# Attention and two expert layers on one core: the second half of a weight product moved behind the first layer and made from float32r parts

## The chip, the cores and the metric

The kernel runs on one core of a Trainium2 chip. The metric is the device time of one execution in microseconds (us). The kernel before was run three times: 860.75, 860.82 and 862.73 us, median 860.82 us.

A core has a matrix engine (TensorE, PE in the profile; its weight loads are PEld), VectorE (DVE), ScalarE (ACT), GpSimd (POOL) and SyncE (SP), which here issues all the transfers. Each engine takes its instructions in the order in which they were written and waits on semaphores for the others.

## The reference

```python
def _attn_ref(q, k, v):                      # 4 batches, 8 heads, 576 positions, 64 wide
    scores = np.matmul(q, k.transpose(0, 1, 3, 2)) / np.sqrt(D)
    # causal mask: 32 wide for heads 0..3, 128 wide with a step of 4 for heads 4..7
    scores = np.where(masks[None], scores, -1000000000.0)
    attn = np.exp(scores - np.max(scores, axis=-1, keepdims=True))
    attn = attn / (np.sum(attn, axis=-1, keepdims=True) + 1e-09)
    return np.matmul(attn, v)

def _moe_ref(x, w1, w2, w3, w_out):          # x 2304x512; w1, w2 512x1024; w3 1024x1024; w_out 1024x512
    a = x @ w1
    b = x @ w2
    h = a * b @ w3
    return h @ w_out

def _moe2_ref(x, w_in, w_out, a, b):         # w_in 512x2048, w_out 2048x512
    h = x @ w_in
    P = a[0] + a[1] * h + a[2] * h * h + a[3] * h * h * h
    Q = 1.0 + np.abs(b[0]) * np.abs(h) + np.abs(b[1]) * h * h
    return (P / (Q + 1e-06)) @ w_out
```

The three are chained: attention gives x, the first expert layer gives a new x, the second the output. The weights arrive as 64-bit words, two int32 each, which are put together on the chip.

## The kernel before

The 2304 tokens go through phase 1 (attention and the first expert layer) in eight blocks of 288 (k = 0..7) and through phase 2 (the second expert layer) in five blocks of up to 512.

Most products run on float32r parts: a number x is cut into a high part (a ScalarE cast) and a low part (VectorE, x minus high), and three products (high by high, high by low, low by high) are summed in PSUM. A plain float32 product needs no parts; it shows in the trace as two matmul records for each instruction.

Phase 1 does not keep w3 and w_out apart. It first forms W3o = w3 w_out (1024 by 512) in two halves of 512 rows, each four PSUM banks, summed over eight slabs j. For each j there are two steps (`w3_mm`, e = 0, 1) of two plain float32 matmuls of 128x512. Each finished bank is then cut into parts (`w3_high`, `w3_low`). The rest is:

- **Slabs.** A weight slab (128x512 words, 512 KB) is loaded, scaled by ScalarE (`scale`, L215), then shifted, signed and completed by VectorE (L219, L223, L234). The eight slabs of w_out and the sixteen of w3 stay whole; the sixteen of w1 and w2 are also cut into parts (`high`, `low`, L241 and L245).
- **Attention.** 32 groups, eight for each pair of blocks. A group is a score product (L316), six masks (L332), six exponentials (L340), sums and a reciprocal (L345, L347), a division on POOL (L352), transposes (L359), a product with v (L374), and its cut into parts (L393, L397).
- **First layer** (`l1`, L426): for each m of 8 and both of w1 and w2, twelve matmuls of 128x288 into the two banks `ab`; then a copy and a product (`l1_copy`, `l1_mul`). The slabs m of w1 and w2 serve blocks 0 and 1 one after the other, so that each slab is used as it comes.
- **Second layer** (`l2`, L472): the product by W3o, for each n of 4 a bank `acc` of 24 matmuls. Block 0's products stay in SBUF as parts (`l1_high`, and `l1_low` on POOL); block 1's go to DRAM (`p_store`), come back (`p_load`) and are cut then (`p_high`, `p_low`).
- **Weights of phase 2.** 32 slabs are put together beside phase 1 and stored in DRAM.

The order of phase 1 is made by a planner (`Plan.order`): every step has an engine, a duration, predecessors, buffers and a due time, and each engine takes the ready step that is due first. The due times come from `main_jobs`, the order of TensorE's products. There it says: first half of W3o, four slabs of the second half, then m by m the first layer of blocks 0 and 1 with one further slab of the second half after each of the first four m, then `l2(0)`, `l2(1)`, then blocks 2 to 7. A first-layer product of block 0 waits for the eight groups of attention of its two blocks and for its slab.

Phase 2 is written out: `step(i)` issues a product with w_in, its rational function, and the product with w_out of four steps earlier. Block 7's second layer is done there (`tail`), after step 0.

Of the kernel before, what the change touches and what calls it, by code (L numbers as in the profile page):

```python
# [18 lines left out]
P = 128  # L19
# [26 lines left out]
W12SLOT = ("p0", "p1", "p2", "p3", "w34", "w35", "w30", "w31",  # L46
           "wo0", "wo1", "wo2", "wo3", "wo4", "wo5", "wo6", "wo7")
# [3 lines left out]
W3BANKS = (("acc", "acc", "ab", "ab"), ("acc", "acc", "sc", "sc"))  # L51
# [4 lines left out]
W3_AT = 4  # L56
PACE = 1.12
B_FROM = 120.0

# [118 lines left out]
class Kern:  # L178
# [28 lines left out]
    def part(self, pool, tag):  # L207
        return pool.tile([P, 2, DM], F32R, tag=tag, bufs=1, name="w")
# [30 lines left out]
    def high(self, s):  # L239
        s["w"] = self.part(s["pool"], s["tag"])  # L240
        self.nc.scalar.copy(s["w"][:, 0], s["x"])  # L241
# [158 lines left out]

    def w3_mm(self, half, j, e):
        if j == 0 and e == 0:
            self.wo[half] = [self.bank(t) for t in W3BANKS[half]]
        w3, wout = self.w3T[half, j]["x"], self.wout[j]["x"]
        for i in (2 * e, 2 * e + 1):
            self.nc.tensor.matmul(self.wo[half][i], w3[:, i * P:(i + 1) * P], wout, start=j == 0,  # L406
                                  stop=j == M1 - 1)
# [42 lines left out]
    def p_store(self, m):  # L450
        self.nc.sync.dma_start(out=self.pd[m // 2, :, m % 2], in_=self.pp[1, m])

    def p_load(self, i):
        w = self.p2[1, i] = self.gp.tile([P, 2, 2, TA], F32R, tag="g", bufs=5, name="pp")
        self.nc.sync.dma_start(out=w[:, 1].bitcast(F32), in_=self.pd[i])

    def p_high(self, i):
        w = self.p2[1, i]
        self.nc.scalar.copy(w[:, 0], w[:, 1].bitcast(F32))

    def p_low(self, i):
        w = self.p2[1, i]
        self.nc.vector.tensor_tensor(out=w[:, 1], in0=w[:, 1].bitcast(F32), in1=w[:, 0].bitcast(F32),
                                     op=ALU.subtract)

    def l2(self, k, n, e):
        if e == 0:
            self.l2_acc[k, n] = self.bank("acc")
        acc = self.l2_acc[k, n]
        for m in range(4 * e, 4 * e + 4):  # L470
            for a, c in ((0, 0), (1, 0), (0, 1)):
                self.nc.tensor.matmul(acc[:, 0:TA], self.W3o[m][0][:, a, n * P:(n + 1) * P],  # L472
                                      self.p2[k, m // 2][:, c, m % 2],
# [30 lines left out]
    def phase1(self):  # L504
        io, Q, Pp = self.io, self.Q, self.Pp
        for n in ("qT", "kT", "vb", "sc", "pr", "sm", "pt", "pT", "xt", "xs", "ab", "a_sb", "pp", "p2",
                  "w3T", "wout", "wo", "w12", "l2_acc", "x2", "bs", "braw", "win", "wo2"):
# [13 lines left out]
        for job in self.main_jobs():  # L521
            T[job] = t
            t += 1.72 if job[0] == "w3" else 1.57 * PACE
# [4 lines left out]
        for G in range(2 * B * HP):  # L528
            u, half = divmod(G, 2)
            b, hp = divmod(u, HP)  # L530
            if half == 0:
                lb = [buf(x) for x in ("qT", "kT", "vb")]
                lq = add("SP", 0.9, self.att_load_q, u, new=lb[0:1])
                lk = add("SP", 0.95, self.att_load_k, u, new=lb[1:2])
                lv = add("SP", 1.2, self.att_load_v, u, new=lb[2:3])
# [5 lines left out]
            due = T["l1", 2 * b, 0, 0] - 1 - (2 * HP - 1 - G % (2 * HP)) * (GAP if b else GAP0)  # L541
# [23 lines left out]
        def words(src, pool, tag, raw=True):  # L565
# [3 lines left out]
            ld = add("SP", 1.6, self.load, s, new=[wb])  # L569
# [13 lines left out]
        keys = [x for j in range(M1) for x in (("o", j), (0, j))] + [(1, j) for j in range(M1)]  # L583
        homes, prev = {}, {}
        for g, j in keys:
            tag = f"wo{j // 2}" if g == "o" else f"wo{4 + j // 2}"
# [4 lines left out]
            s, a = unsplit(src, n, homes[hk], xbs[hk], Q, tag, prev[hk])  # L591
# [7 lines left out]
        w3o, last = [], []  # L599
        for g in range(2):  # L600
            wb = [buf(x) for x in W3BANKS[g]]
            for j in range(M1):
                for e in range(2):
                    f = j == 0 and e == 0
                    a = add("PE", 1.72, self.w3_mm, g, j, e, after=[ready["o", j], ready[g, j]] + last[-1:],
                            new=wb if f else [], use=([] if f else wb) + [xbs["o", j // 2], xbs[g, j // 2]],
                            due=T["w3", g, j, e])
                    last = [a]
            for i in range(4):
                hi = add("ACT", 0.6, self.w3_high, g, i, after=last + w3o[-1:], new=[buf(f"p{4 + 4 * g + i}")],  # L610
                         use=[wb[i]], due=T["w3", g, M1 - 1, 1] + 2 + 0.6 * i)
                w3o.append(hi)
                last.append(add("DVE", 0.66, self.w3_low, g, i, after=[hi], use=[wb[i]],
                                due=T["w3", g, M1 - 1, 1] + 3 + 0.6 * i))
            lows = last[1:] if g == 0 else lows + last[1:]
            last = last[:1]
# [17 lines left out]
        def l1_jobs(k, m):  # L634
# [13 lines left out]
            if k == 1:  # L648
                kept[m] = add("SP", 0.45, self.p_store, m, after=[mu], use=tb[1:], due=d + 4)
# [8 lines left out]
        def back_jobs():  # L658
            pl, gbs = parts.setdefault(1, ([], []))
            for i in range(M1 // 2):  # L660
                gb = buf("g")
                d = T["l2", 1, 0, 0] - 12 + 1.5 * i
                a = add("SP", 0.95, self.p_load, i, new=[gb], due=d,
                        after=[kept[2 * i], kept[2 * i + 1]] + parts[0][0][-1:])
                a = add("ACT", 0.67, self.p_high, i, after=[a], use=[gb])
# [355 lines left out]
```

## Time and profile before

| | |
|---|---|
| median of 3 runs | 860.82 us |
| the profiled execution, time | 860.87 us |
| its span, first to last instruction | 859.1 us |
| TensorE busy | 838.7 us (98%) |
| VectorE busy | 578.5 us (67%) |
| ScalarE busy | 533.7 us (62%) |
| mean granted TensorE clock | 0.998 |

The profiled execution is one run of the program; 1.8 us of its time lie outside its span. Busy time is the time in which an engine executes; a line such as L426 is the line of the source from which the instruction was issued. A tile is named without its number, and its four uses as PSUM bank are `ab`, `acc`, `sc` and `px`, two banks each.

### The profile page before, as it was taken

How to read it: one execution, taken by the hardware profiler on the slowest of the kernel's cores; microseconds unless marked ns; L12 is line 12 of the kernel's file. 1: busy time of each engine (PE TensorE's matmuls, PEld its weight loads, DVE VectorE, ACT ScalarE, POOL GpSimd, SP SyncE). 2: the span in 40 equal slices, each digit the busy share in tenths (PEclk: the TensorE clock that was granted, in tenths of full speed). 3: DMA queues.
4: the chain of work that ended last, by engine and by line, in shares of the span. 5: the costliest groups of instructions: out<-in, count | busy, mean ns of one | idle time of the engine just before them, and what ended most of it. 6: DMA issues, size and time to landing. Idle time of an engine off the chain costs nothing.

```text
span 859.1 us, 14509 instructions
## 1 busy us (share of the span) xinstructions
PE 838.7 (98%) x5216; PEld 718.1 (84%) x5216; DVE 578.5 (67%) x1264; ACT 533.7 (62%) x1202; POOL 328.1 (38%) x305
## 2 busy tenths in 40 slices
PE   5989999999999999999999999999999999999998
PEld 2546799889999999999998778888888888888886
DVE  6889997776775223321225887788777877787775
ACT  3785557663566334632235877777777777787773
POOL 1240023132143213312123655565556655564443
PEclk9999999999999999999999999999999999999999
DMA  9787346876775112042334000010000100001112
GB/s 357 257 334 238 114 135 220 291 251 221 256 256 166 54 56 77 19 150 104 105 107 145 25 14 24 12 38 14 26 13 24 37 13 13 13 25 42 43 45 93
DMA packets 43464, 95.06 MB, mean 111 GB/s; under 512 B 4736, under 2 KB 13952, under 8 KB 43392
## 3 DMA queue, kind: packets, MB, share of 16 engines
q1 hardware_dynamic: 43392, 94.13, 32.5%
q8 instruction: 41, 0.67, 0.3%
q14 instruction: 31, 0.25, 0.1%
HBM read 71.57 MB, written 22.54 MB: 110 GB/s over the span
## 4 chain that ended last, share of the span: by engine, by line
PE 89%; ACT 5%; DVE 4%; DMA 1%; issue 1%; POOL 0%; SPq 0%; ACTq 0%; POOLq 0%; DVEq 0%
PE ab L426 24%; PE acc L851 11%; PE sc L851 11%; PE ab L801 11%; PE px L801 10%; PE acc L472 10%; PE acc L406 3%; PE sc L316 2%; PE px L374 2%; PE sc L406 2%; PE px L359 2%; PE ab L406 1%; DMA words<-moe_w_in 1%; ACT pr L340 1%; DVE v L829 1%
## 5 line engine op out<-in xcount | busy, mean ns | idle before, releaser
L426 PE MATMUL ab<-xs,w 128*128 128x288 f32 x1536 | 215.9, 298 | 0.2 <-ACT xs L393 0.2
L426 PEld LDWEIGHTS ab<-xs,w 128*128 128x128 f32 x1536 | 205.8, 188 | 5.4 <-issue 1.7
L812 POOL TENSOR_TENSOR y<-y,v 128x512 f32<-128x512 f32 x72 | 95.8, 1331 | 143.1 <-ACT y L811 142.8
L352 POOL TENSOR_TENSOR pr<-pr,sm 96x384 f32<-96x384 f32 x64 | 56.3, 898 | 175.0 <-DVE sm L347 124.3
L851 PE MATMUL acc<-w,gg 128*128 128x512 f32 x432 | 109.7, 391 | 1.4 <-ACT r L822 1.4
L472 PE MATMUL acc<-pp,w 128*128 128x288 f32 x768 | 109.2, 298 | 1.2 <-DVE XS L909 1.0
L447 POOL TENSOR_TENSOR pp<-p,pp 128x288 fp32r<-128x288 f32 x56 | 48.1, 860 | 162.7 <-ACT pp L443 156.1
L851 PE MATMUL sc<-w,gg 128*128 128x512 f32 x432 | 109.4, 390 | 0.0
L472 PEld LDWEIGHTS acc<-pp,w 128*128 128x128 f32 x768 | 103.3, 188 | 2.9 <-PE acc L472 1.2
L801 PE MATMUL ab<-XS,w 128*128 128x512 f32 (+1 forms) x480 | 105.4, 370 | 0.0
L801 PE MATMUL px<-XS,w 128*128 128x512 f32 (+1 forms) x480 | 105.3, 370 | 0.0
L838 POOL TENSOR_TENSOR gg<-t,gg 128x512 fp32r<-128x512 f32 x72 | 93.7, 1302 | 10.7 <-ACT gg L837 10.1
L801 PEld LDWEIGHTS px<-XS,w 128*128 128x128 f32 x480 | 83.8, 188 | 16.4
L801 PEld LDWEIGHTS ab<-XS,w 128*128 128x128 f32 x480 | 83.7, 188 | 16.2
L851 PEld LDWEIGHTS acc<-w,gg 128*128 128x128 f32 x432 | 80.7, 188 | 19.2 <-ACT r L822 1.8
L851 PEld LDWEIGHTS sc<-w,gg 128*128 128x128 f32 x432 | 80.8, 188 | 17.3
L436 DVE TENSOR_TENSOR p<-a_sb,ab 128x288 f32<-128x288 f32 x64 | 28.9, 452 | 81.2 <-PE ab L426 68.4
L340 ACT ACTIVATE pr<-pr,sm 96x128 f32<-96x128 f32 x192 | 74.8, 395 | 9.0 <-DVE sm L332 9.0
L215 ACT ACTIVATE dec<-words 128x512 f32<-128x512 f32 x72 | 47.9, 676 | 37.9 <-DMA words<-moe_w_out 11.8
L829 DVE SCALAR_TENSOR_TENSOR v<-y,cs,r 128x512 f32<-128x512 f32 x72 | 71.2, 989 | 0.0
L821 ACT ACTIVATE r<-y,cs 128x512 f32<-128x512 f32 x72 | 52.2, 726 | 14.5 <-POOL y L812 14.3
L811 ACT ACTIVATE y<-v,cs 128x512 f32<-128x512 f32 x72 | 58.8, 817 | 2.4
(76 smaller groups left out, 1152.9 us busy)
## 6 DMA issues: line engine op xcount, KB each, us to landing
words<-moe_w SPq DMA_DIRECT2D x32, 512.0 KB, 5.3
words<-moe_w_out SPq DMA_DIRECT2D x24, 512.0 KB, 4.5
words<-moe_w_in SPq DMA_DIRECT2D x16, 512.0 KB, 4.1
wd<-dec SPq DMA_DIRECT2D x32, 256.0 KB, 2.3
c<-wd SPq DMA_DIRECT2D x32, 256.0 KB, 2.6
vb<-v SPq DMA_DIRECT2D x16, 384.0 KB, 3.7
XS<-x2d SPq DMA_DIRECT2D x6, 1024.0 KB, 7.6
kT<-k SPq DMA_DIRECT2D x16, 304.0 KB, 4.2
```

Of the source, the lines that this page charges most:

```text
L340: self.nc.scalar.activation(out=pr[:, i], in_=pr[:, i], func=AF.Exp, scale=-1.0, bias=sm[:, 0, i:i + 1], accum_out=sm[:, 1, i:i + 1])
L352: self.nc.gpsimd.tensor_tensor(out=pr[:, i], in0=pr[:, i], op=ALU.mult, in1=sm[:, 2, i].unsqueeze(2).to_broadcast([QT, 3, P]))
L406: self.nc.tensor.matmul(self.wo[half][i], w3[:, i * P:(i + 1) * P], wout, start=j == 0, stop=j == M1 - 1)
L426: self.nc.tensor.matmul(t[:, 0:TA], w[:, s[0], c * P:(c + 1) * P], xs[:, s[1], c, tok], start=n == 0, stop=n == 11)
L472: self.nc.tensor.matmul(acc[:, 0:TA], self.W3o[m][0][:, a, n * P:(n + 1) * P], self.p2[k, m // 2][:, c, m % 2], start=m == 0 and (a, c) == ...
L801: nc.tensor.matmul(t[:, e * nt:(e + 1) * nt], w[:, s[0], c * P:(c + 1) * P], XS[blk][:, s[1], c], start=n == 0, stop=n == 11)
L811: nc.scalar.activation(out=w, in_=v, func=AF.Identity, scale=self.b1, bias=self.b0)
L812: nc.gpsimd.tensor_tensor(out=w, in0=w, in1=v, op=ALU.mult)
L821: nc.scalar.activation(out=r, in_=yy[i][1], func=AF.Ln, bias=self.c1)
L829: nc.vector.scalar_tensor_tensor(out=v, in0=w, scalar=self.c1, in1=r, op0=ALU.add, op1=ALU.mult)
L838: nc.gpsimd.tensor_tensor(out=t[:, 1], in0=u, in1=t[:, 0].bitcast(F32), op=ALU.subtract)
L851: nc.tensor.matmul(acc[g, blk][tk], t[:, s[0], j:j + P], w[:, s[1]], start=f + e == 0 and s == (0, 0), stop=f + e == FG - 1 and s == (1, 0))
```

## The change

The second half of W3o is no longer computed in plain float32 before and between the first layer's products. It comes after the first layer of blocks 0 and 1, and its two operands are cut into parts: w_out's slab j once more (`wout_high`, `wout_low`, whole slabs from the first half being kept) and w3's slab (`high`, `low`). For each bank three float32r matmuls take the place of one float32 matmul. The parts live in the ring `g` of five buffers.

Since `g` is taken, block 0's products now go to DRAM as block 1's did, and come back when the last w_out part is made; `l1_high` and `l1_low` are no longer issued for block 0. `l2` goes over n in two passes of two banks: for each pair of m, both n of the pass. The second pass uses the banks `ab` in phase 1 and `sc` in the tail of phase 2, where the first uses `acc`. w_out's whole slabs live in other slots, so that eight of the sixteen w1 and w2 slabs can be made early. In phase 2 the product with w_out takes the token rows first and the slabs inside (for the last block of 256 tokens alone this makes a difference). Five of the planner's numbers are changed; the attention of blocks 0 and 1 is due earlier.

```diff
-W12SLOT = ("p0", "p1", "p2", "p3", "w34", "w35", "w30", "w31",
-           "wo0", "wo1", "wo2", "wo3", "wo4", "wo5", "wo6", "wo7")
+W12SLOT = ("p0", "p1", "p2", "p3", "wo0", "wo1", "wo2", "wo3",
+           "w34", "w35", "w30", "w31", "wo4", "wo5", "wo6", "wo7")
-W3BANKS = (("acc", "acc", "ab", "ab"), ("acc", "acc", "sc", "sc"))
+W3BANKS = ("acc", "acc", "ab", "ab")
-W3_AT = 4
-PACE = 1.12
+AHEAD = 1.0
+PACE = 1.15
+L2BANKS = (("acc", "ab"), ("acc", "sc"))
...
     def w3_mm(self, half, j, e):
...
+            for a, c in SPLIT:
+                self.nc.tensor.matmul(out, self.w3T[1, j]["w"][:, a, r], self.woutp[j][:, c],
+                                      start=j == 0 and (a, c) == (0, 0), stop=j == M1 - 1 and a == 1)
+
+    def wout_high(self, j):
+        w = self.woutp[j] = self.gp.tile([P, 2, DM], F32R, tag="g", bufs=5, name="woutp")
+        self.nc.scalar.copy(w[:, 0], self.wout[j]["x"])
+
+    def wout_low(self, j):
+        w = self.woutp[j]
+        self.nc.vector.tensor_tensor(out=w[:, 1], in0=self.wout[j]["x"], in1=w[:, 0].bitcast(F32),
+                                     op=ALU.subtract)
...
-    def l2(self, k, n, e):
+    def l2(self, k, h, i):
+        ns = (2 * h, 2 * h + 1)
+        if i == 0:
+            for n in ns:
+                self.l2_acc[k, n] = self.bank(L2BANKS[k == NA - 1][h])
+        order = [(m, n) for m in (2 * i, 2 * i + 1) for n in ns]
+        if i == M1 // 2 - 1:
+            order.sort(key=lambda x: x[1])
+        for m, n in order:
...
-            if k == 1:
-                kept[m] = add("SP", 0.45, self.p_store, m, after=[mu], use=tb[1:], due=d + 4)
+            if k < 2:
+                kept[k, m] = add("SP", 0.45, self.p_store, k, m, after=[mu], use=tb[1:], due=d + 4)
...
+        def second(j):
+            src = io["moe_w3"][1, j]
+            s, wb, db, a = words(src, Q, f"w3{2 + j % 2}")
...
+            a = hi = add("ACT", 0.63, self.high, s, after=[a] + chain, new=[pb], use=[db])
+            lo = add("DVE", 0.64, self.low, s, after=[a], use=[db, pb], port=True)
+            a = add("ACT", 0.63, self.wout_high, j, after=[ready["o", j], hi], new=[gb], use=[xbs["o", j // 2]])
+            chain[:] = [a]
+            a = split[0] = add("DVE", 0.64, self.wout_low, j, after=[a], use=[gb, xbs["o", j // 2]], port=True)
+            return [lo, a], [pb, gb]
...
-        jobs = w3(0, range(M1)) + w3(1, range(W3_AT))
+        jobs = w3(0, range(M1))
         for i in range(M1):
-            jobs += l1(0, [i]) + l1(1, [i]) + (w3(1, [W3_AT + i]) if W3_AT + i < M1 else [])
-        jobs += l2(0) + l2(1)
+            jobs += l1(0, [i]) + l1(1, [i])
+        jobs += w3(1, range(M1)) + l2(0) + l2(1)
```

Where the products stand on TensorE is shown at three places. The first is the start of the program. Before (L406 is a step of W3o, L316 a group's score product, L359 its transposes, L374 its product with v):

```order
L406 MATMUL acc<-x 128x512 x2
L406 MATMUL ab<-x 128x512 x2
L406 MATMUL acc<-x 128x512 x2
L406 MATMUL ab<-x 128x512 x2
L406 MATMUL acc<-x 128x512 x2
L316 MATMUL sc<-kT,qT 96x128 x6
L406 MATMUL ab<-x 128x512 x2
L406 MATMUL acc<-x 128x512 x2
```

The same place of the changed kernel (L412 is the float32 step, L319, L362 and L377 are the attention's three):

```order
L319 MATMUL sc<-kT,qT 96x128 x12
L412 MATMUL acc<-x 128x512 x2
L362 MATMUL px<-ident,pr 128x96 x3
L412 MATMUL ab<-x 128x512 x2
L362 MATMUL px<-ident,pr 128x96 x3
L319 MATMUL sc<-kT,qT 96x128 x6
L377 MATMUL px<-pT,vb 64x96 x6
L412 MATMUL acc<-x 128x512 x2
```

Attention now comes first, and its groups are spread over the sixteen steps of the first half. The second place is the first layer of blocks 0 and 1. Before:

```order
L426 MATMUL ab<-xs,w 128x288 x48
L406 MATMUL acc<-x 128x512 x2
L406 MATMUL sc<-x 128x512 x2
L426 MATMUL ab<-xs,w 128x288 x12
L406 MATMUL acc<-x 128x512 x2
L406 MATMUL sc<-x 128x512 x2
L406 MATMUL acc<-x 128x512 x2
L406 MATMUL sc<-x 128x512 x2
L426 MATMUL ab<-xs,w 128x288 x96
```

After (L445 is the first layer, L416 the second half of W3o from parts):

```order
L377 MATMUL px<-pT,vb 64x96 x6
L445 MATMUL ab<-xs,w 128x288 x300
L319 MATMUL sc<-kT,qT 96x128 x6
L445 MATMUL ab<-xs,w 128x288 x84
L362 MATMUL px<-ident,pr 128x96 x6
L319 MATMUL sc<-kT,qT 96x128 x6
L416 MATMUL acc<-woutp,w 128x512 x6
L416 MATMUL ab<-woutp,w 128x512 x6
L416 MATMUL acc<-woutp,w 128x512 x6
L377 MATMUL px<-pT,vb 64x96 x6
```

The first layer runs through without a step of W3o between its products, and the sixteen steps behind it are six matmuls each. The third place is the end of phase 1 and the tail of phase 2 (L472 is the second layer, L801 the product with w_in). Before:

```order
L472 MATMUL acc<-pp,w 128x288 x96
L426 MATMUL ab<-xs,w 128x288 x192
L801 MATMUL ab<-XS_4706,w 128x512 x12
L472 MATMUL acc<-pp,w 128x288 x96
L801 MATMUL ab<-XS_4706,w 128x512 x12
```

After (L496 is the second layer, L843 the product with w_in):

```order
L496 MATMUL acc<-pp,w 128x288 x48
L496 MATMUL ab<-pp,w 128x288 x48
L445 MATMUL ab<-xs,w 128x288 x192
L843 MATMUL ab<-XS_4816,w 128x512 x12
L496 MATMUL acc<-pp,w 128x288 x48
L496 MATMUL sc<-pp,w 128x288 x48
L843 MATMUL ab<-XS_4816,w 128x512 x12
```

Block 6's second pass sits in `ab`, which block 7's first layer takes next; block 7's second pass sits in `sc`, where all four n were in the two banks `acc`.

## Rows read from the trace of the kernel before

**Rows 1.** The page, busy time of each engine and the chain's shares.
```profile
PE 838.7 (98%) x5216; PEld 718.1 (84%) x5216; DVE 578.5 (67%) x1264; ACT 533.7 (62%) x1202; POOL 328.1 (38%) x305
...
PE 89%; ACT 5%; DVE 4%; DMA 1%; issue 1%; POOL 0%; SPq 0%; ACTq 0%; POOLq 0%; DVEq 0%
```

**Rows 2.** Waits of TensorE: line, releaser: us in total, times, longest.
```profile
PE acc L406 <- DVE x L234: 8.7, 1, 8.7
...
PE px L359 <- POOL pr L352: 1.7, 2, 1.3
...
PE acc L472 <- DVE XS L909: 1.0, 1, 1.0
```

**Rows 3.** The chain in order of time: start us, us, what.
```profile
0.75 3.54 DMA words<-moe_w_out
...
57.30 2.93 PE acc L406 x4
60.23 2.23 PE sc L406 x4
62.45 1.72 PE acc L406 x4
...
78.06 6.39 PE ab L426 x48
...
190.18 14.22 PE ab L426 x108
...
503.57 2.72 PE px L801 x12
```

**Rows 4.** TensorE by line, the attention's three products, all 32 groups.
```profile
L316 PE MATMUL sc<-kT,qT 64*96 64x128 f32 x384 | 30.3, 283 | 2.0 <-DVE sm L332 1.9
L359 PE MATMUL px<-ident,pr 96*128 96x96 f32 x192 | 24.6, 249 | 2.9 <-POOL pr L352 1.7 <-DVE xs L397 1.3
L374 PE MATMUL px<-pT,vb 128*64 128x96 f32 x384 | 23.2, 255 | 0.2 <-ACT pT L365 0.2
```

**Rows 5.** Stretches: length, busy PE, PEld, DVE, ACT, POOL; clock, DMA, GB/s.
```profile
5.00:78.00 73.00, 66.46 (x341) 34.39 (x342) 63.96 (x204) 48.34 (x155) 15.18 (x16) 0.98 0.83 305
...
58.00:59.00 1.00, 1.00 (x2) 0.33 (x1) 0.97 (x3) 1.00 (x7) 0.00 (x0) 0.50 0.99 406
...
78.00:190.00 112.00, 109.44 (x857) 97.48 (x856) 94.91 (x264) 68.84 (x210) 24.94 (x26) 1.00 0.63 204
```

**Rows 6.** VectorE in order of time: start us, us, instruction [idle before it].
```profile
5.00 0.43 DVE L219 TENSOR_SCALAR dec<-dec 128x512 int32<-128x512 int32 x1 [5.00 <-ACT dec L215]
...
6.80 0.42 DVE L219 TENSOR_SCALAR dec<-dec 128x512 int32<-128x512 int32 x1
...
20.83 0.29 DVE L332 CUSTOM_DVE_ANT_0 pr<-sc,masks 96x128 f32<-96x128 f32 x1 [2.17 <-PE sc L316]
...
78.61 0.69 DVE L245 TENSOR_TENSOR w<-dec,w 128x512 fp32r<-128x512 f32 x1
79.21 0.68 DVE L234 SCALAR_TENSOR_TENSOR x<-words,dec 128x512 int32<-128x512 int32 x1
```

**Rows 7.** VectorE by line, the masks: busy us, mean ns of one, idle before.
```profile
L332 DVE CUSTOM_DVE_ANT_0 pr<-sc,masks 96x128 f32<-96x128 f32 x192 | 43.0, 281 | 10.7 <-PE sc L316 9.8 <-POOL pr L352 0.7
```

**Rows 8.** ScalarE by line, in the same columns.
```profile
L340 ACT ACTIVATE pr<-pr,sm 96x128 f32<-96x128 f32 x192 | 74.8, 395 | 9.0 <-DVE sm L332 9.0
...
L481 ACT CAST x<-acc 128x288 fp32r<-128x288 f32 x28 | 11.3, 402 | 32.3 <-PE acc L472 25.3 <-PE px L359 2.8 <-issue 2.1
...
L241 ACT CAST w<-dec 128x512 fp32r<-128x512 f32 x16 | 9.9, 619 | 9.4 <-DVE dec L234 9.4
```

**Rows 9.** TensorE in the tail of phase 2, block 7's second layer.
```profile
446.18 6.55 PE L472 MATMUL acc<-pp,w 128*128 128x288 f32 x48
453.70 6.63 PE L472 MATMUL acc<-pp,w 128*128 128x288 f32 x48 [0.98 <-DVE XS L909]
```

**Rows 10.** VectorE's last instructions, the last block's two output tiles.
```profile
854.82 1.37 DVE L864 TENSOR_TENSOR X<-sc,X 128x512 f32<-128x512 f32 x2 [4.07 <-PE sc L851]
```

More of the change, by code (lines that the diff above doesn't have):

```diff
@@ L402, in w3_mm @@
         if j == 0 and e == 0:
-            self.wo[half] = [self.bank(t) for t in W3BANKS[half]]
-        w3, wout = self.w3T[half, j]["x"], self.wout[j]["x"]
+            self.wo[half] = [self.bank(t) for t in W3BANKS]
         for i in (2 * e, 2 * e + 1):
-            self.nc.tensor.matmul(self.wo[half][i], w3[:, i * P:(i + 1) * P], wout, start=j == 0,
-                                  stop=j == M1 - 1)
+            r, out = slice(i * P, (i + 1) * P), self.wo[half][i]
+            if half == 0:
+                self.nc.tensor.matmul(out, self.w3T[0, j]["x"][:, r], self.wout[j]["x"], start=j == 0,
+                                      stop=j == M1 - 1)
+                continue
+            for a, c in SPLIT:
[8 more added lines that the diff above has]
+                                     op=ALU.subtract)
     def w3_high(self, half, i):
@@ L568, in words @@
             wb, db = buf(tag), buf(f"dec{self.nd % 2}")
-            ld = add("SP", 1.6, self.load, s, new=[wb])
+            ld = add("SP", 1.35, self.load, s, new=[wb])
             a = add("ACT", 0.68, self.scale, s, after=[ld], new=[db], use=[wb])
@@ L598, in phase1, with w3_jobs @@
             n += 1
-        w3o, last = [], []
-        for g in range(2):
-            wb = [buf(x) for x in W3BANKS[g]]
+        lows = []
+        def w3_jobs(g, begin, data, work):
+            wb = [buf(x) for x in W3BANKS]
+            last = begin
             for j in range(M1):
+                after, bufs = data(j)
                 for e in range(2):
                     f = j == 0 and e == 0
[L605 to L608, printed above, removed]
+                    last = [add("PE", work, self.w3_mm, g, j, e, after=after + last, new=wb if f else [],
+                                use=([] if f else wb) + bufs, due=T["w3", g, j, e])]
+            d = T["w3", g, M1 - 1, 1]
             for i in range(4):
[L610 to L616, printed above, removed]
+                hi = add("ACT", 0.6, self.w3_high, g, i, after=last + lows[-1:], new=[buf(f"p{4 + 4 * g + i}")],
+                         use=[wb[i]], due=d + 2 + 0.6 * i)
+                lows.append(add("DVE", 0.66, self.w3_low, g, i, after=[hi], use=[wb[i]], due=d + 3 + 0.6 * i))
+            return last
+        w3_jobs(0, [], lambda j: ([ready["o", j], ready[0, j]], [xbs["o", j // 2], xbs[0, j // 2]]), 1.72)
         w12, w12b = {}, {}
@@ L688, in phase1 @@
                 l1_jobs(k, m)
-        l2_jobs(0)
-        back_jobs()
-        l2_jobs(1)
+        def second(j):
+            src = io["moe_w3"][1, j]
+            s, wb, db, a = words(src, Q, f"w3{2 + j % 2}")
+            self.w3T[1, j] = s
+            s.update(wpool=self.gp, wtag="g")
+            a = add("DVE", 0.66, self.low_bits, s, after=[a], use=[db, wb], port=True)
+            pb, gb = buf("g"), buf("g")
+            a = hi = add("ACT", 0.63, self.high, s, after=[a] + chain, new=[pb], use=[db])
[4 more added lines that the diff above has]
+            return [lo, a], [pb, gb]
+        split, chain = [None], []
+        l1s += w3_jobs(1, l1s[-1:], second, 1.37)
+        for k in range(2):
+            back_jobs(k)
+            l2_jobs(k)
         for k in range(2, NA):
@@ L916, in phase2 @@
         step(0)
-        for n in range(KC):
-            tail(n)
+        for h in range(2):
+            tail(h)
         for i in range(1, N + LAG):
```

118 lines of the change are left out of this document (57 added, 61 removed).

## The prediction

> **What bounds the kernel now.** I read the page first: TensorE is busy for 98% of the span and the chain that ended last is 89% TensorE [rows 1]. So a change is worth what it does to TensorE's work and to the few places where TensorE stands still. The list of its waits shows where these are [rows 2]: 8.7 us at the start, until VectorE has put the first two slabs together; small ones in the attention; and 1.0 us in the tail. Then the chain in order of time [rows 3] gives the milestones: the first layer begins at 78.06 and block 2's first layer at about 190. From there to the end the change moves almost nothing but the tail. Last, the stretches [rows 5]: up to 78 VectorE is busy for 63.96 of 73 us, while from 78 to 190 TensorE is busy for 109.4 of 112. So the first 78 us are shared between TensorE and VectorE, and the next 112 us belong to TensorE.
>
> **Term A, TensorE's work.** The second half is 16 steps. A float32 step takes 1.72 us when nothing disturbs it (at 62.45) [rows 3]; 16 x 1.72 = 27.5 us. A step now has six float32r matmuls of 128x512. Twelve of these, in phase 2, take 2.72 us (at 503.57) [rows 3], so a step takes 1.36 and sixteen 21.8. The second layer keeps its number of matmuls, as does the first. A is -5.8 us.
>
> **Term B, the start.** Before the first layer's first product the kernel before does 25 float32 steps and eight groups of attention. A group costs TensorE 0.95 + 0.77 + 0.72 = 2.44 us (30.3, 24.6 and 23.2 us over 32 groups) [rows 4], so this is 43.0 + 19.5 = 62.5 us of work by 78.06: 15.5 us lost, with the first wait, later gaps and a cold stretch (below). Now there are 16 steps and the same eight groups: 47.1 us of work. The question is when it can end, and VectorE decides that, since the first layer waits for the eighth group's low part.
>
> VectorE's work ahead of that low part follows from the count of its instructions in either order. Before: 25 slabs put together, three w1 or w2 slabs cut, four W3o banks cut, eight groups; together the 63.96 us busy by 78 [rows 5], with a few tenths of the next slab. After: 19 slabs and the beginning of a 20th, two slabs and three banks cut, the same eight groups. A slab takes 1.80 us (from one shift to the next, 5.00 to 6.80) and a cut 0.60 (78.61 to 79.21; the bank's cut has the same shape) [rows 6]. So the work falls by 6 x 1.80 - 0.4 + 2 x 0.60 = 11.6 us to 52.4. VectorE's first work is now a mask, which waits for kT, qT and a score product: the first load of 512 KB lands at 4.3 [rows 3], these two are 592 KB, and the product adds 0.95; I take 5.2 again.
>
> What is left is VectorE's idling. Before it was 9.0 us between 5 and 78 [rows 5]. The bounds: none (start of the first layer at 57.6, still later than TensorE's own 47.1 + 4.3), and the 9.0 once more or a few us above, since the attention and the slabs now take turns from the start. I take 7.4, near the row: the same handovers occur, less the 2.2 us in which the first masks waited for a score product that stood behind five steps (at 20.83) [rows 6], plus some for slabs that now queue behind kT and qT. The first layer begins at 5.2 + 52.4 + 7.4 = 65.0. TensorE has then lost 65.0 - 47.1 = 17.9 us instead of 15.5. B is +2.4 us, with -5 and +4 as its ends.
>
> **Term C, from the first layer to block 2.** Before, 2.5 us are lost in 112 [rows 5]. Now the sixteen slabs of w1 and w2 must keep up with a first layer without pauses: for each m TensorE works 6.4 us (48 products in 6.39) [rows 3] and VectorE 2 x (1.80 + 0.60) + 2 x 0.4 = 5.6, so they do, with four ready at the start. Then VectorE makes the parts of the second half. From the last first-layer product to the last pair of parts its order has five slabs, eleven cuts and two groups of attention: 9.0 + 6.6 + about 4 (masks 43.0 us over 32 groups [rows 7], and half as much again for sums and parts) = 19.6. TensorE comes to that pair after 14 steps and three groups' pieces, 19.0 + 7.4 = 26.4. So 6.8 us are to spare, and the loads of block 0's products start when that pair is made, well before TensorE asks for them. The tightest place is the fourth part of the second layer's first pass, which needs the last W3o bank and the fourth load; there VectorE has 34 us of work by its order against TensorE's 37.7. I expect stalls of 2.0 us in all: C is -0.5, bounded by -2.5 (none) and +3.
>
> **Term D, the tail.** Block 7's third n waited 0.98 us for a bank `acc` to be emptied [rows 9]. It now goes into `sc`, which nothing holds. VectorE and ScalarE have the same pieces to empty. D is -1.0; if the following steps, which wait on VectorE, eat it up, it is 0.
>
> **Term E, banks.** Block 7's first layer takes `ab` right behind block 6's second pass. The last part is sorted by n, so the first bank is done 6 x 0.133 = 0.8 us before the pass ends (48 in 6.39) [rows 3]; emptying takes 0.40 us on ScalarE [rows 8], about as long on VectorE and two handovers, some 1.2 in all. E is +0.4. At the other blocks the order puts pieces of attention there. For the last block the new loop order lets the first output tile be emptied earlier, but the second still waits for the last product, and VectorE was waiting for TensorE there [rows 10]: 0.
>
> Sum: -5.8 + 2.4 - 0.5 - 1.0 + 0.4 = -4.5. From the profiled execution's 860.87 us (859.1 and 1.8 around it) this gives 856.4; the median of the runs is 860.82, which changes nothing. A difference of 0.3%, 2.6 us, is about what can be told from none.
>
> **The clock.** From 58 to 59 the granted clock was 0.50 [rows 5], that is 1.2 instead of 2.4 GHz, right after TensorE had stood for some 1.3 us behind POOL's division [rows 2] and a few shorter gaps; the two steps there took 2.93 and 2.23 us instead of 1.72 [rows 3], 1.7 us lost. The changed start has more standing still. The Trainium skill ("TensorE: Matmul & The Clock Gate", section "HAM oscillation — how this bites in real kernels") says that a matmul loop which pauses for its operands falls back to the slow clock at every pause and runs each burst cold. By that rule the start would lose its 1.7 us again and again; the trace agrees with the fall, but shows it once, after several gaps together.
>
> **Rivals.**
>
> 1. *The start takes it all.* VectorE idles 11.6 instead of 7.4 us, because in-order ScalarE and VectorE wait for each other in every group. For: before, it idled 9.0 with fewer groups early. Against: the work itself fell by 11.6. Time 856.4 + 4.2 = 860.6.
> 2. *The ring turns too slowly* (slower than before). Five buffers hold two slabs' parts and one more. The parts of j + 2 can be made only when j's products are done: two casts of 0.62 [rows 8] and two cuts of 0.60, behind exponentials (three take 1.2) [rows 8] and masks (six take 1.3) [rows 7] in order: 2.4 to 4.9 us against the 2.7 us of j + 1's two steps, and about 0.9 of attention between. If each of six turns loses 1.3 us, the time is 856.4 + 7.8 = 864.2. It is slower from 1.2 us a turn on (4.5 + 2.6 over six). Against: VectorE's spare 6.8 us, and one buffer ahead.
> 3. *The clock falls at the first layer too, twice more than before*: 2 x 1.7 = 3.4, 859.8.
> 4. *A better start*: VectorE idles 4 us, and no stalls behind: 856.4 - 3.4 - 2.0 = 851.0.
>
> **How the numbers follow.** The forecast 0.50 (its own range 853.5 to 859), rival 1 0.22, rival 2 0.09, rival 3 0.07, rival 4 0.12. Faster by over 0.3% means under 858.2: most of the forecast (0.44), rival 4 (0.12) and some 0.04 of rivals 1 and 3: 0.60. Slower, above 863.4: rival 2 and a bad end of rival 1, 0.10. The rest, 0.30, is the same. The range from 852 to 862 leaves out the low half of rival 4 and rival 2.
>
> **What would show it.** In the changed trace: the sixteen steps of the second half in 1.36 us each; the first layer's first product near 65 us; VectorE idle about 7 us until then; block 2's first layer about 121.5 us after the first layer began; no wait at block 7's third n. If the first layer begins after 68, B is wrong; if waits on L416 add up to over 3 us, it is the ring; granted clock of 0.50 beyond one short stretch would be rival 3.

## The result and the profile after

The changed kernel is slower: 867.94 us median (866.22 to 869.20, 4 runs) against 861.24 of the kernel before (4 runs), ratio 1.0073 (95% interval 1.0055 to 1.0090). 856.4 was predicted, with a range from 852 to 862. The profiled execution took 868.17, its span 866.4.

First the page of the changed kernel, busy time and the chain's shares [rows 1].

```profile
PE 839.6 (97%) x5248; PEld 731.0 (84%) x5248; DVE 593.1 (68%) x1284; ACT 541.3 (62%) x1214; POOL 320.8 (37%) x297
...
PE 85%; DVE 5%; DMA 4%; ACT 4%; issue 1%; POOL 0%; SPq 0%; DVEq 0%; ACTq 0%; POOLq 0%
```

TensorE is not busy for less time than before, but for 0.9 us more, and DMA now holds 4% of the chain instead of 1%. Where the time went is told by the stretches between the milestones: first layer, block 2's, block 4's, block 7's second layer, end (columns as in [rows 5]).

```profile
0.00:63.29 63.29, 50.17 (x304) 28.59 (x305) 51.88 (x183) 45.10 (x150) 16.50 (x31) 0.98 0.96 360
63.29:189.17 125.88, 122.02 (x936) 112.26 (x936) 107.93 (x288) 77.61 (x219) 14.84 (x16) 0.98 0.52 170
189.17:291.97 102.80, 98.74 (x816) 94.06 (x816) 70.24 (x207) 55.84 (x184) 28.47 (x32) 0.97 0.67 219
291.97:454.47 162.50, 162.08 (x1285) 157.17 (x1285) 46.06 (x167) 61.41 (x196) 39.80 (x48) 0.99 0.27 89
454.47:866.40 411.93, 406.61 (x1909) 338.89 (x1907) 316.97 (x442) 301.35 (x468) 221.21 (x170) 1.00 0.12 39
```

Three of the same stretches of the kernel before:

```profile
190.02:284.82 94.80, 94.77 (x818) 90.76 (x816) 62.01 (x187) 52.13 (x167) 25.37 (x30) 1.00 0.67 219
284.82:446.18 161.36, 161.19 (x1299) 156.43 (x1298) 40.62 (x169) 61.22 (x200) 38.41 (x48) 1.00 0.23 75
446.18:859.10 412.92, 406.86 (x1909) 339.00 (x1907) 316.95 (x442) 301.19 (x468) 221.18 (x170) 1.00 0.12 39
```

| milestone, us | before | predicted | after |
|---|---|---|---|
| first layer | 78.06 | 65.0 | 63.29 |
| block 2's first layer | 190.02 | 186.1 | 189.17 |
| block 4's first layer | 284.82 | 280.9 | 291.97 |
| block 7's second layer | 446.18 | 442.7 | 454.47 |
| end of the span | 859.1 | 854.6 | 866.4 |

The predicted milestones behind the first one are those of before plus the terms of the sum; the 121.5 us that the prediction names between the first two would put block 2 at 186.5.

So the first layer begins 1.7 us earlier than forecast, block 2's begins 3.1 us later, and 8.0 us more are lost between blocks 2 and 4, where the prediction let nothing happen: before, TensorE stood for 0.03 us there, now for 4.06, and its work there takes 4 us longer at a mean clock of 0.97.

The waits of TensorE (line, releaser: us in total, times, longest) [rows 2]:

```profile
PE sc L319 <- DVE sm L335: 4.5, 5, 1.7
PE sc L319 <- DMA qT<-q: 4.4, 1, 4.4
PE acc L412 <- DVE x L237: 3.8, 1, 3.8
PE px L377 <- ACT pT L368: 2.5, 4, 1.8
PE ab L445 <- ACT a_sb L451: 2.1, 1, 2.1
PE px L362 <- POOL pr L355: 1.9, 3, 1.4
PE ab L445 <- DVE w L435: 1.7, 1, 1.7
...
PE ab L445 <- DVE x2l L509: 0.3, 1, 0.3
```

No L416 among them: the ring of parts (rival 2) never held TensorE up. At the head of block 4 one sees how such a wait comes about. ScalarE, VectorE and TensorE, each in order of time:

```profile
285.95 1.25 ACT L218 ACTIVATE dec<-words 128x512 f32<-128x512 f32 x2 [4.25 <-DMA words<-moe_w_in]
...
288.87 0.69 ACT L396 CAST xs<-px 128x288 fp32r<-128x288 f32 x1 [0.80 <-PE px L377]
```

```profile
286.65 0.43 DVE L222 TENSOR_SCALAR dec<-dec 128x512 int32<-128x512 int32 x1 [4.53 <-ACT dec L218]
...
289.75 0.28 DVE L335 CUSTOM_DVE_ANT_0 pr<-sc,masks 96x128 f32<-96x128 f32 x1
...
291.02 0.68 DVE L400 TENSOR_TENSOR xs<-px,xs 128x288 fp32r<-128x288 f32 x1
```

```profile
290.52 0.46 PE L319 MATMUL sc<-kT,qT 64*96 64x128 f32 x2 [1.69 <-DVE sm L335]
291.15 0.89 PE L319 MATMUL sc<-kT,qT 64*96 64x128 f32 x10 [0.18 <-DVE sm L335]
291.97 2.94 PE L445 MATMUL ab<-xs,w 128*128 128x288 f32 x12
```

ScalarE stood 4.25 us in front of a slab of phase 2 that had not landed, VectorE 4.53 behind it. Then the slabs' own work ran, then masks and the group's low part (291.02), and only behind that the first layer. Neither engine may take the attention first: the order is fixed. The two other long waits of that kind are at block 2's head and in block 3. TensorE at both, and ScalarE ahead of the second:

```profile
187.59 0.46 PE L319 MATMUL sc<-kT,qT 64*96 64x128 f32 x2 [1.54 <-DVE sm L335]
...
189.17 2.61 PE L445 MATMUL ab<-xs,w 128*128 128x288 f32 x12
...
265.08 3.25 PE L445 MATMUL ab<-xs,w 128*128 128x288 f32 x12 [2.09 <-ACT a_sb L451]
```

```profile
261.76 0.68 ACT L218 ACTIVATE dec<-words 128x512 f32<-128x512 f32 x1 [2.35 <-DMA words<-moe_w_in]
```

Ahead of the copy `a_sb` ScalarE had stood 2.35 us for another slab of phase 2. The scale's line over all 72 slabs (after, then before) shows that before, the last slab was scaled 20 us ahead of block 4's head, and that now the last comes 17 us behind it:

```profile
L218 ACT ACTIVATE dec<-words x72: 644/674/708, 7.8 to 308.9; 128x512 f32<-128x512 f32 x72
```

```profile
L215 ACT ACTIVATE dec<-words x72: 655/676/692, 4.3 to 264.6; 128x512 f32<-128x512 f32 x72
```

At block 2's head 23 of the 72 were left to scale, 18 before. Between blocks 2 and 4 ScalarE stood 15.4 us for loads of slabs, 10.7 before, the longest 4.3 and 2.2 us. So it stood for slabs before as well, but at places where TensorE lost next to nothing (0.03 us).

The clock pays a second time. Four stretches of the changed kernel, where before had one short one [rows 5]:

```profile
61.00:67.00 6.00, 4.26 (x21) 3.96 (x18) 5.97 (x12) 3.75 (x8) 0.00 (x0) 0.50 0.64 233
190.00:194.00 4.00, 4.00 (x25) 3.44 (x24) 3.31 (x15) 2.97 (x14) 0.96 (x2) 0.58 0.99 349
265.00:269.00 4.00, 3.92 (x19) 3.91 (x20) 2.50 (x15) 1.04 (x4) 2.81 (x3) 0.57 0.44 169
292.00:296.00 4.00, 4.00 (x25) 3.68 (x24) 2.17 (x16) 1.89 (x10) 1.61 (x2) 0.57 0.88 275
```

Half of TensorE's busy time at 0.50, 1.2 GHz, is lost: 2.4 us in the first (from 60.4 on) and 1.7 in each other, 7.5 in all against 1.7 before. These rows miss the program's beginning. There they show 1.00, yet the first products are slow: four records of the same form took 3.46 us at 12.88 and 1.91 at 16.43.

```profile
12.88 3.46 PE L412 MATMUL acc<-x 128*128 128x512 f32 x4 [3.76 <-DVE x L237]
...
16.43 1.91 PE L412 MATMUL ab<-x 128*128 128x512 f32 x4
```

By the lengths of its records TensorE is slow up to 13.3 us before and up to 15.9 after. It works 4.6 and 6.8 us in that time; at half speed that is 2.3 and 3.4 us lost, 1.1 more than before.

The account up to block 7's second layer: idle +7.2 (21.5 against 14.3; 1.6 at the start, 1.3 up to block 2, 4.0 up to block 4, 0.3 behind), clock +5.8 by the rows, the rest of TensorE's busy time -4.7, in all +8.3; the tail -1.0. In the -4.7 are the 1.1 us of the slow beginning; without them the products gain 5.8.

### The profile page after: what moved, and what is told of

The parts are those of the page before. It is cut to its first block, busy times and chain, and to the rows that moved or that the text cites. A ratio compares the mean times of both kernels' runs of the same rounds, so it can differ in the third digit from the quotient of the medians.

```text
span 866.4 us, 14638 instructions
## 1 busy us (share of the span) xinstructions
PE 839.6 (97%) x5248; PEld 731.0 (84%) x5248; DVE 593.1 (68%) x1284; ACT 541.3 (62%) x1214; POOL 320.8 (37%) x297
## 4 chain that ended last, share of the span: by engine, by line
PE 85%; DVE 5%; DMA 4%; ACT 4%; issue 1%; POOL 0%; SPq 0%; DVEq 0%; ACTq 0%; POOLq 0%
PE ab L445 23%; PE acc L893 11%; PE sc L893 11%; PE ab L843 11%; PE px L843 10%; PE acc L496 5%; PE ab L496 3%; PE sc L319 2%; DMA words<-moe_w_in 2%; PE px L377 2%; PE px L362 2%; PE acc L412 2%; PE ab L416 1%; PE acc L416 1%; DMA words<-moe_w_out 1%; PE ab L412 1%
## 5 line engine op out<-in xcount | busy, mean ns | idle before, releaser
L445 PE MATMUL ab<-xs,w 128*128 128x288 f32 x1536 | 216.4, 301 | 4.3 <-ACT a_sb L451 2.1
L445 PEld LDWEIGHTS ab<-xs,w 128*128 128x128 f32 x1536 | 209.8, 192 | 7.8 <-ACT a_sb L451 2.3
L843 PE MATMUL ab<-XS,w 128*128 128x512 f32 (+1 forms) x480 | 105.4, 369 | 0.0
L843 PE MATMUL px<-XS,w 128*128 128x512 f32 (+1 forms) x480 | 105.3, 370 | 0.0
L843 PEld LDWEIGHTS px<-XS,w 128*128 128x128 f32 x480 | 83.8, 188 | 16.4
L843 PEld LDWEIGHTS ab<-XS,w 128*128 128x128 f32 x480 | 83.7, 188 | 16.2
L466 POOL TENSOR_TENSOR pp<-p,pp 128x288 fp32r<-128x288 f32 x48 | 41.3, 861 | 100.6 <-ACT pp L462 100.4
L462 ACT CAST pp<-p 128x288 fp32r<-128x288 f32 x48 | 20.8, 433 | 55.0 <-DVE p L455 55.0
L226 DVE SCALAR_TENSOR_TENSOR dec<-words,dec 128x512 int32<-128x512 int32 x72 | 53.8, 755 | 1.7
```

Source lines behind the costliest of these rows:

```text
L226: self.nc.vector.scalar_tensor_tensor(out=s["d"], in0=s["words"][:, :, 1], scalar=-0x80000000, in1=s["d"], op0=ALU.bitwise_and, op1=ALU.bi ...
L445: self.nc.tensor.matmul(t[:, 0:TA], w[:, s[0], c * P:(c + 1) * P], xs[:, s[1], c, tok], start=n == 0, stop=n == 11)
L843: nc.tensor.matmul(t[:, e * nt:(e + 1) * nt], w[:, s[0], c * P:(c + 1) * P], XS[blk][:, s[1], c], start=n == 0, stop=n == 11)
```

## The experiments

T1 says that slabs which land later than planned hold the in-order engines, and with them the attention. T2 says that the parts made behind the first layer crowd VectorE and ScalarE there. T3 says that the planner's order is a draw, and any change of its numbers moves such waits.

**Planned load times.** The change also lowered four planned times of SP's loads. e1 puts them back; e4 gives the new ones to the kernel before.

```diff
-lq = add("SP", 0.75, ...    # k 0.8, v 1.0        e1, changed kernel; e4 is the reverse, kernel before
-ld = add("SP", 1.35, self.load, s, new=[wb])
+lq = add("SP", 0.9, ...     # k 0.95, v 1.2
+ld = add("SP", 1.6, self.load, s, new=[wb])
```

> The changed kernel with the planner's four load times set back to those of before (0.9, 0.95, 1.2 and 1.6 us for q, k, v and a slab). Theory 1 (slabs land later than planned, ScalarE and VectorE stand in order before them, TensorE waits and then runs at 1.2 GHz): a slab is planned to land 0.25 us later, a small part of the 0.4 to 3.6 us by which the four on the chain were late; 867.9 falls by 1 to 3 us, to 865 to 867. Theory 2 (the parts of the second half crowd VectorE, so that more phase-2 slabs are left for the stretch from 190 to 300): no change, 867 to 869.

> The kernel before with the planner's four load times of the changed kernel (0.75, 0.8, 1.0 and 1.35 us). Theory 1: slabs are waited for in order here too: 1 to 4 us slower, 862 to 865. Theory 2: 860 to 862.

e1: 871.6 us, ratio 1.0108 (1.0079 to 1.0138), slower still: both theories missed. e4: 866.4, 1.0060 (1.0044 to 1.0075): the four numbers alone cost the kernel before 5 us, more than T1 had said, and at another place: its first layer begins at 95.9, with 16.2 us idle ahead of it instead of 11.5 and a second cold stretch. At equal planned times the changed kernel is slower by 1.5 us (new times: 867.9 and 866.4) and by 10.3 (old times: 871.6 and 861.3).

**Phase 2's slabs planned to land late** (e2), and **the second half in plain float32** at its new place (e3).

```diff
-ld = add("SP", 1.35, self.load, s, new=[wb])                 # e2; without tail it is 2.0
+ld = add("SP", 1.35, self.load, s, new=[wb], tail=tail)      # 5.5 for phase 2's slabs
```

e3 makes no parts of the second half, multiplies `w3T[1, j]["x"]` by `wout[j]["x"]` as the first half does, and plans 1.72 us a step.

> The changed kernel, with the planner told that a phase-2 slab lands 5.5 us after its issue instead of 2.0; nothing else. Theory 1: the waits of 1.5, 2.1 and 1.7 us before blocks 2 and 4 and in block 3, and the three stretches at 1.2 GHz behind them (1.7 us each), go: 867.9 - 5.3 - 5.1 = 857.5, at least below 862. Theory 2: the slabs are as many, VectorE is as busy: 865 to 869.

> The changed kernel, with the second half of W3o in plain float32 at its new place: no parts, 16 steps of 1.72 instead of 1.36 us. It uses float32 products where the changed kernel uses three float32r ones. Theory 1: TensorE's work is 5.8 us more, the late slabs stay: 870 to 874. Theory 2: VectorE is freed of 16 cuts (9.7 us) and more phase-2 slabs are done before block 2: the waits go with their cold stretches, 867.9 + 5.8 - 10.4 = 863.

e2: 865.94, 1.0058 (1.0040 to 1.0076): T2's number. A later plan alone gives back 2 us (the intervals overlap), not the 10 of T1. e3: 875.93, 1.0162 (1.0141 to 1.0183), 2 us above T1's range and 13 above T2's number. The parts are worth 8.0 us against plain products at the same place, 5.8 of them by term A; the rest can be the other order. In e3 the last slab is scaled at 297.9, ahead of block 4's head (304.2), and the time is higher all the same: T2 falls as the cause.

**The slabs taken away, the clock held up, the tail alone, one number changed.**

```diff
-s, wb, db, a = words(src, Q, f"w3{2 + i % 2}")                                          # e5
+s, wb, db, a = words(src, Q, f"w3{2 + i % 2}", since=(184.0 if i < FC else 282.0) + 4.5 * (i % FC))
...
+for i in range(12):                       # e6, at the end of att_pv(15), att_pv(23), att_qk(22)
+    self.nc.tensor.matmul(t[:, 0:TA], self.W3o[0][0][:, 0, 0:P], self.W3o[1][0][:, 0, 0:TA], start=i == 0, stop=i == 11)
...
-self.l2_acc[k, n] = self.bank("acc")                                                    # e7, kernel before
+self.l2_acc[k, n] = self.bank("sc" if k == NA - 1 and n > 1 else "acc")
...
-ld = add("SP", 1.35, self.load, s, new=[wb])                                            # e9
+ld = add("SP", 1.40, self.load, s, new=[wb])
```

> The changed kernel with the 32 slabs of phase 2 given to the planner in two windows, 16 from 184 us on (behind block 2's first layer in the plan) and 16 from 282 us on (behind block 4's), one per 4.5 us. Nothing is computed otherwise. T1 (slabs that land later than planned hold in-order ScalarE and VectorE, and with them the attention ahead of blocks 2 and 4): the waits of 1.5 us ahead of block 2 and of 1.7 us ahead of block 4 and the cold stretches behind them go, some 3.5 us each, and perhaps the 2.1 us at 265 with its cold stretch too: 857 to 861 us, block 2's first layer some 122.5 us after the first one. T3 (the planner's order is what it is, and any change of its numbers only moves such waits): waits of the same size elsewhere, 864 to 870 us.

> The changed kernel in the same order, with 12 more products of 128x288 (1.6 us of work whose result nothing reads) put into TensorE's order at three places at which it waited 1.5, 2.1 and 1.7 us: ahead of the scores whose wait precedes block 2's and block 4's first layer, and ahead of block 3's last m of the first layer. If the clock's fall behind a wait is a price of its own (T1's second half): granted clock 1.0 at 190 to 194, 265 to 269 and 292 to 296 us, the first layer's twelve there in 1.6 instead of 2.6 to 3.3 us; 5 to 6 us less, 862 to 863 us. If the twelve are slow because their operands come late and not for the clock (rival): the 4.8 us of added work lie in the waits and the time stays at 867 to 869 us.

> The kernel before with one thing changed: the third and fourth n of block 7's second layer go into banks sc instead of acc. If the tail's term (D) of the prediction is right: no wait of 0.98 us there, 860.3 us against 861.3. If the steps behind it eat it up: 861.3.

> The changed kernel with the planner's time for a slab's load 1.40 instead of 1.35 us, 4% more; what is computed stays. T1: the loads still land later than planned, nothing is cured: 866 to 868.5 us. T3: the waits fall elsewhere and the time moves by 2 us or more in either direction.

e5: 860.30, 0.9978 (0.9964 to 0.9993), in T1's range, and under the kernel before. TensorE at block 4's head in e5 (the kept execution took 863.08, the longest of its seven):

```profile
282.95 0.90 PE L319 MATMUL sc<-kT,qT 64*96 64x128 f32 x12
283.78 6.40 PE L445 MATMUL ab<-xs,w 128*128 128x288 f32 x46
```

No wait there, and no slow first twelve products of the first layer, where 1.87 us and a cold stretch had been. The windows are worth 7.6 us by the medians. That this is what the slabs ahead of blocks 2 and 4 had cost is not shown: e5 is also another order, with waits of its own (1.48 us at 196.79; 1.17 at 331.22, with a cold stretch behind it), and below, e9 gains 5.2 us with block 2's wait in place, while e15 frees both heads and gains 3.8.

e6: 866.23, 1.0054 (1.0035 to 1.0074); 862 to 863 was expected. TensorE at block 2's head in e6 (L314 is the added work):

```profile
189.00 1.85 PE L314 MATMUL acc<-w 128*128 128x288 f32 x12
190.78 1.36 PE L325 MATMUL sc<-kT,qT 64*96 64x128 f32 x12
192.20 1.85 PE L455 MATMUL ab<-xs,w 128*128 128x288 f32 x12
```

The first layer's twelve take 1.85 instead of 2.61 us, and the granted clock is 1.00 at 190 to 194, 265 to 269 and 292 to 296 us: the clock is what made them slow, and the rival falls. The gain stayed at 1.7 (the intervals overlap), since the added 5.5 us of work filled waits of nearly that length and new waits came (1.07 us at 200.88, 0.57 at 269.28).

e7: 860.17, 0.9987 (0.9976 to 0.9997), 1.1 us less; the second pass starts without a wait [rows 9]:

```profile
445.82 6.55 PE L472 MATMUL acc<-pp,w 128*128 128x288 f32 x48
452.21 6.56 PE L472 MATMUL sc<-pp,w 128*128 128x288 f32 x48
```

e9: 862.74, 1.0007 (0.9997 to 1.0016). T1's 866 to 868.5 missed, T3 hit: 4% on one planned time is 5 us. Its block 2 has the very wait of the changed kernel (1.54 and 0.18 us at L319), and this time the clock stayed up:

```profile
189.76 0.46 PE L319 MATMUL sc<-kT,qT 64*96 64x128 f32 x2 [1.54 <-DVE sm L335]
190.40 0.89 PE L319 MATMUL sc<-kT,qT 64*96 64x128 f32 x10 [0.18 <-DVE sm L335]
191.34 1.85 PE L445 MATMUL ab<-xs,w 128*128 128x288 f32 x12
```

**More draws**: the slab's planned load time alone, at 1.55 and 1.65 in the kernel before, at 1.30 and 1.45 in the changed one.

```diff
-ld = add("SP", 1.6, self.load, s, new=[wb])     # kernel before
+ld = add("SP", 1.55, self.load, s, new=[wb])    # e10; e11 1.65; e12 and e13 1.30 and 1.45 in the changed kernel
```

> The kernel before with the planner's time for a slab's load 1.55 instead of 1.60 us, 3% less; what is computed stays. T3 (the order that the planner writes is a draw: small changes of its numbers move the in-order waits and the cold stretches by several us): the time moves by up to 5 us, and more likely up than down, since 1.60 is the value that was kept: 861 to 866 us, with new waits of over 1 us between 78 and 290 us. T1 (only the loads that land late in the changed kernel's order count): 861.5 us, as before.

> The kernel before with the planner's time for a slab's load 1.65 instead of 1.60 us, 3% more; what is computed stays. T3: 861 to 866 us, as with 1.55, in other places. T1: 861.5 us.

> The changed kernel with the planner's time for a slab's load 1.30 instead of 1.35 us, 4% less; what is computed stays. T3: another draw, 860 to 869 us; with the draws at 1.35 (867.9) and 1.40 (862.7) the kernels of this change lie about as high as the draws of the kernel before do. T1 (the earlier a slab is planned, the more the loads come late): 868 to 870 us.

> The changed kernel with the planner's time for a slab's load 1.45 instead of 1.35 us, 7% more; what is computed stays. T3: another draw, 860 to 869 us. T1 (with 1.40 at 862.7, a later planned landing cures a part each time): 859 to 862 us.

e10: 862.35, 1.0005 (0.9993 to 1.0017). e11: 858.87, 0.9963 (0.9948 to 0.9978). e12: 863.94, 1.0027 (1.0013 to 1.0042). e13: 866.88, 1.0062 (1.0040 to 1.0083). e11 is faster than the kernel before by a number that computes nothing, below what either theory said; e10, e12 and e13 lie in T3's ranges, e12 and e13 outside T1's, and e10 fits both. The changed kernel's four orders (1.30 to 1.45) lie between 1.0007 and 1.0073, mean 1.0042; the other's three between 0.9963 and 1.0005, mean 0.9989. So either kernel scatters by 0.4 to 0.7%, and the means differ by 0.5%: "as high as the draws of before" did not hold for these. With e1 and e4, which change four of these numbers, the ranges overlap (1.0007 to 1.0108, and 0.9963 to 1.0060), and the means (1.0055 and 1.0007) still differ by 0.5%.

**Pairs with the same rule for the slabs.** T4: the change gains by itself, but the slabs cost it more than they cost before. T5: it costs by itself.

```diff
+since=(186.0 if i < FC else 282.0) + 4.5 * (i % FC)    # e14, kernel before
+since=(184.0 if i < FC else 282.0) + 2.8 * (i % FC)    # e15, changed kernel
+since=(186.0 if i < FC else 282.0) + 2.8 * (i % FC)    # e16, kernel before
```

> The kernel before with phase 2's 32 slabs in the two windows (16 from 186 us on, 16 from 282 us on in the plan, one per 4.5 us), as the changed kernel had them in the run where they cost it least (860.3 us). T4 (the change itself gains, but it leaves VectorE and ScalarE less room ahead of blocks 2 and 4, so that phase 2's slabs there cost it more than they cost before): before gains little, 859 to 862 us, and with the slabs out of the way the changed kernel is no slower than it. T5 (the change costs by itself, whatever the slabs do): before gains as much as the changed kernel did (7 us): 853 to 856 us.

> The changed kernel with phase 2's slabs in two denser windows (one per 2.8 us from 184 and from 282 us on), so that more of them lie where no attention is made. T4: no waits of over 1 us at block 2's and block 4's first layer, 857 to 861 us. T3 (a draw like the others): 860 to 868 us.

> The kernel before with the same denser windows (from 186 and from 282 us on). T4: 859 to 862 us, at least as much as the changed kernel with them. T5: 4 us or more below the changed kernel with them.

e14: 859.01, 0.9965 (0.9950 to 0.9979). e15: 864.17, 1.0027 (1.0011 to 1.0043). e16: 859.81, 0.9982 (0.9970 to 0.9993). By the medians the kernel before gains 3.0 and 2.2 us, the changed one 7.6 and 3.8. That fits T4's first half, that the slabs cost it more, though each is a new order too; yet with the windows it is still 0.13% (within the intervals) and 0.45% above the other. T4's second half, no slower than the other, fails in the second pair. In e15 no wait precedes the first layer at the heads of blocks 2 and 4, as T4 said, but its 857 to 861 us did not come. T5's 853 to 856 us for e14 did not come either; its 4 us between e15 and e16 did (4.4 by the medians, 0.45%).

**The second layer n by n** at blocks 1 to 6, as before, with the changed kernel's planned times (e17), with e5's windows (e18), and at 1.45 (e19). T6: the second pass ends with two `ab` banks full at once, in front of the first layer and the attention.

```diff
+for n in range(KC if k else 0):
+    ab = buf("acc")
+    for e in range(2):
+        a = l2s[k] = add("PE", 1.57, self.l2n, k, n, e, ...
...
-for h in range(2):
+for h in range(0 if k else 2):
```

> The changed kernel with the second layer of blocks 1 to 6 one n at a time in the two banks acc, as the kernel before has it; block 0 and block 7 keep the two passes of two n each. T6 (the second pass ends with two banks full at once in the first layer's own banks ab, so that the first layer waits for them and four pieces of ScalarE and VectorE stand together at each block's head, ahead of the attention's): no wait of the first layer on a half cut from ab (0.3 to 2.7 us in every order of the changed kernel), shorter waits at blocks 2 and 4, 3 to 6 us less: 861 to 865 us. T5 in another form (the passes cost nothing, the change's other parts do): 866 to 869 us.

> The same with phase 2's slabs in the two windows (one per 4.5 us) in which the changed kernel took 860.3 us and the kernel before 859.0. T6: 2 to 4 us less than with the two passes, 856 to 858.5 us, at or below the kernel before with the same windows. T5: 859.5 to 861.

> The same as the first, at the planner's load time of 1.45 us, at which the changed kernel took 866.9. T6: 3 to 6 us less, 861 to 864 us. T5: 865 to 868.

e17: 864.41, 1.0036 (1.0022 to 1.0049). e18: 859.11, 0.9971 (0.9958 to 0.9984). e19: 866.73, 1.0058 (1.0040 to 1.0077). Against the kernels with two passes and the same planned numbers: -3.2, -0.6 and -0.3 us, the last two within the intervals. The waits on `x2l` at the first layer (0.3 to 2.7 us in the orders with two passes) are gone in all three, others took their place; T6's range holds in e17 alone (e18 lies between the two theories, e19 in T5's range), and it is not the common cause. e18 is the best order of the changed kind, 0.9971, not to be told from e14 (0.9965) and e11 (0.9963), the best of the other; all three beat the kernel before and the changed one. The stretches of e14 and e18 up to block 7's second layer, e14 first:

```profile
0.00:444.49 444.49, 430.82 (x3308) 378.75 (x3309) 261.48 (x822) 232.82 (x734) 107.15 (x135) 1.00 0.53 178
```

```profile
0.00:443.39 443.39, 427.24 (x3340) 387.19 (x3341) 273.97 (x842) 239.37 (x746) 96.58 (x127) 0.99 0.54 183
```

TensorE stands 16.15 us in e18, 13.67 in e14 (+2.5, of which 2.0 ahead of the first layer). It works 3.6 us less, with 0.7 more lost to the clock at the start. That leaves 1.1 us, and the tail 1.0, of the 4.5 forecast, in one execution each; the medians don't show it.

## Why the prediction was wrong

- **A held.** The sixteen steps run in 1.36 us each when nothing stands between them; here two of the changed kernel's, begun 1.36 apart. With the lines of the first half the products of w3 w_out fell from 65.3 to 57.9 us, 1.7 of it the kernel before's cold steps and 0.8 its slow beginning, where six of its products were slow and three of the changed kernel's. That leaves 4.9 by this count and 5.8 by the account above, the size that was forecast.

```profile
126.53 1.52 PE L416 MATMUL ab<-woutp,w 128*128 128x512 f32 x6
127.89 1.52 PE L416 MATMUL acc<-woutp,w 128*128 128x512 f32 x6
```

- **B held in its milestone, not in its price.** The first layer began at 63.3 to 65.2 in all twelve orders with the new start and the second half from parts; 65.0 was forecast. In the changed kernel VectorE worked 51.9 us up to it (52.4 forecast) and idled 6.2 from 5.2 us on (7.4 forecast). But the cold stretch runs on past that moment (to 67), some 0.7 us more lost than before, which a milestone doesn't show; the slow beginning takes 1.1 more, inside the milestone.
- **C failed**, and with it the sentence ahead of it, that from block 2 to the end the change moves almost nothing but the tail. C put 121.5 us between the first layer and block 2's, and 125.9 were taken: 3.9 us of stalls for the 2.0 expected, and 1.9 for the clock, which C put at nothing. Then 8.0 more went up to block 4, a stretch put at nothing: 4.0 of waits, 3.4 for the clock behind them. The sum counted how much work VectorE has by a moment. The planner wrote another order of the same pieces, in which phase 2's slabs stand ahead of the attention at the heads of blocks 2 and 4 and ahead of a copy in block 3. What counts there is which instruction stands in front and whether its load has landed. e5, with the slabs in windows, is 7.6 us faster; how much of that is these slabs' and how much the new order's is not shown.
- **D held**: -1.0 in the profile, 1.1 alone in e7.
- **E** was 0.25 us at block 7 in every order with two passes, 0.4 forecast. At the other blocks, where E expected none, the changed kernel had no such wait either, but other orders of it had up to 2.5 us (e12).
- **Rival 3 was priced too low.** It gave two more falls, 3.4 us, and had them at the first layer. Three came at later stages and a longer one at the start, 5.8 us more than before by the clock's rows. The rule of the Trainium skill ("TensorE: Matmul & The Clock Gate", section "HAM oscillation — how this bites in real kernels"), that a loop falls to the slow clock at its pauses, deserved more than 0.07. The trace agrees at four places, and e9 disagrees at one: the same pause of 1.54 us, no fall. The Trainium skill tells it of a kernel with longer pauses (3 to 5 us) than the waits behind which the clock fell here (1.5 to 2.1 us).
- **The chances.** 0.10 for slower left no room for a case that the account needs: another order with other waits. The range of 10 us is wider than what 3 to 7% on one planned time does to either kernel (862.7 to 867.9, and 858.9 to 862.4), but it was laid around a sum that put this scatter at nothing, and it reached only 5.6 us up.

What stays open: why the changed kernel's orders lie higher as a group. Its start is part of it (2.0 us more idle in e18 than in e14, and 0.7 more for the clock). Behind the start the kept traces differ too: between the first layer and block 7's second layer TensorE stands 1.6 to 5.2 us in the seven orders of the kernel before (itself, e4, e7, e10, e11, e14, e16), 5.0 to 9.8 in the ten of the changed kernel with two passes, and 2.8 to 7.5 in e17 to e19. What it waits for differs from order to order (`x2l`, `p`, `a_sb`, masks), and the orders run are too few to say which part of the change makes them. The other parts (the due times, the slots of the slabs, block 0's products by way of DRAM) were not taken back one by one.

## What to carry to other kernels

Where a planner writes the order, a change of the work is also a new draw of the order. Price both: run two or three neighbouring values of a number that computes nothing before a difference of 0.5% is put down to the change. In fixed orders look at what stands ahead of each stage's first product on the engines behind it; a load that is not urgent does not belong there, and a bound on when it may start, with the new order that came of it, moved this kernel by 7.6 and 3.8 us and the one before by 3.0 and 2.2.

## What was not expected of the hardware

The same wait of TensorE (1.54 us, then scores with 0.18 us between them, then twelve products) was followed by the slow clock in the changed kernel (2.61 us for the twelve) and not in e9 (1.85). A fall cost 1.7 to 2.4 us in the changed kernel. Twelve idle-filling products kept the clock up in e6 at all three places.
